# 16-bit sine phases built by doubling, sines in four pieces, and a second written order of the front

## The chip, the cores and the metric

The kernel runs on one NeuronCore of one Trainium2 chip. The metric is the device time of one execution in microseconds, from the first to the last instruction and what lies around them. Lower is better.

## The reference

The inputs are sequences of S = 2048 positions with D = 448 channels in bfloat16. What is computed, cut to what matters:

```python
def _A_ref(q, k, v, shift_k, ssm_k, ssm_D):
    k_shift = sum(k_pad[:, t:t + S, :] * shift_k[:, 3 - t] for t in range(4))    # four taps
    kv = k_shift * v
    y = irfft(rfft(kv_pad, axis=1) * rfft(kf_pad, axis=1))[:S] + kv * ssm_D      # causal convolution, length 4096
    return q * y

x = A_q
h = x + _A_ref(_layernorm(x), A_k, A_v, A_shift_k, A_ssm_k, A_ssm_D)
h2 = h + _B_ref(_layernorm(h), B_w1, B_b1, B_w2, B_b2)    # layernorm, @w1 over S, +b1, gelu, @w2, +b2, transposed
```

## The kernel before

**The Fourier transform as matmuls.** The 2048 positions are laid out as 128 partitions (q) times 16 rows (r). The convolution is done with a two-stage transform. Its factors are sine and cosine values of phases in units of 1/8192 turn. Each factor table is made in the kernel: an integer phase is built on VectorE (DVE), and ScalarE (ACT) takes its sine. The large table is `E`, 128 partitions by 32 times 128 values in float16; its upper half serves rows 8 to 15, its lower half rows 0 to 7. The small tables `FW`, `MA`, `MB`, `MN` serve the second stage and its inverse.

**The steps.** Each operation belongs to a step with a name: the emitting function's tag, a running number, and after a colon the operation's index in the step.
- `dummy`: matmuls without use on PE at the start; `kT.1:9-11` and `kT.3:9-11` are three more each.
- `tables`: `tables.0` iotas on POOL, two memsets and a first Sin activation of one column on ACT (L785); `tables.1` and `tables.3` the identity matrix (L789, L810, L812); `tables.2` further iotas; `tables.4` sixteen memsets on POOL and five operations of up to eight columns on DVE (L822 to L831), the last of which (`tables.4:20`) gives the column scalars that the small tables need; `tables.5` and `tables.6` the phases and the sine of each half of `E` (L837, L841, L844, L847); `tables.7` the small tables (POOL L854 x3 and L858, DVE L860, ACT L862, DVE L866 x2, POOL L871 x3 and L874). After the change the steps that make `E` are `tables.5` to `tables.8`, and the small tables are `tables.9`, with the same indices.
- `loads`: the inputs from HBM: `KN` (A_ssm_k, L887, four transfers), `KH` (A_k, L898, four), `V` (A_v, L901, four), the rest small.
- `kT.0` to `kT.7`: transposes of `KN` on PE (L1037), two steps for each of the four transfers, each copied out of PSUM by an evacuation (L738 on ACT, L741 on DVE).
- `kv.1` to `kv.8`: transposes of `KH` (L965), and their evacuations. `kv.9` to `kv.16`: the four-tap shift as matmuls (L991), each with two multiplications by `V` on DVE (L1006).
- `k1` and `u1` (16 steps each): the first stage (L1058) for the filter and for kv. Each step fills two PSUM banks, is evacuated as 128x896 (L1068; `k1.0` to `k1.3` as an addition on DVE, L1066), and every second step sends three transfers that shuffle partitions, two issued by POOL and one by SP (L1074).
- `k2` and `u2` (8 pairs each): the second stage (L1093), evacuated by ACT or DVE (L739, L742; L738, L741).
- `i1`: 16 products on DVE (L1160), the inverse's matmuls (L1177), their evacuations, and shuffling transfers (L1201, L1188).
- `q`, `xn`: mean and variance of x (`bn_stats` L1237, L1239) and the normalised first rows.
- `ct0`, `ct`: transposes of `E` for the last stage (L1107), each with an evacuation; `ct0` also copies factors (L1126).
- `i2`: the last inverse stage (L1309), the gate, and the second layernorm (L1319 to L1388).
- `mlp`: L1435 and L1445 (w1), Gelu L1425, and L1457 (w2), with the output added on DVE (L1460).

**What sets the order.** The order is written out by hand in `ORDER`: for each of the five engines one list of operations, and an engine works its list from the first to the last. `SLOTS` writes out which of the eight PSUM banks and of the rings of buffers in SBUF each step takes. A planner's model goes through the lists only to emit the instructions; the waits come from what each operation reads and writes. A waiting instruction therefore holds up all that stands behind it on its engine, and transfers stand in the list of the engine that issues them: POOL issues two of three shuffling transfers among its computations. The order about the front's start is, on POOL, `tables.4`'s memsets, `tables.1:0`, `tables.0:1`, `tables.0:2`; on DVE

```
"dummy.0:0 tables.3:0-1 kv.0:3 tables.6:0 tables.4:16 tables.5:0 tables.4:17 tables.6:1 tables.4:18 "
"tables.5:1 tables.4:19 tables.6:2 tables.4:20 tables.5:2 kT.1:8 tables.7:6 kT.0:8 kT.3:8 tables.7:4 "
```

## Time and profile before

| what | value |
|---|---|
| three runs | 170.51, 170.92, 170.98 us; median 170.92 |
| profiled execution, its own time | 170.65 us |
| its span, first to last instruction | 168.8 us |
| granted TensorE clock | 1.000 |
| busy: PE, DVE, ACT, POOL | 160.0, 101.9, 90.4, 58.4 us |

The profiled execution takes 1.85 us more than its span, and the median of the runs is 0.27 us above it. In a row of the timeline stand the start in us, the length, the engine, the line, the operation, the operands' shapes and a count; a merged row holds several equal instructions. In a row of groups stand the count, the busy time in us and the mean of one in ns. In a row of the chain stand start, length, and what was done. In a table by stages stand the stretch, its length, and each engine's busy time.

### The profile page before, as it was taken

What the parts mean: (1) busy time and instruction counts of PE and PEld (TensorE: products, weight loads), DVE (VectorE), ACT (ScalarE), POOL (GpSimd) and SP (SyncE); (2) the same over time, 40 slices, a digit from 0 to 9 for tenths busy, and PEclk for the clock granted to TensorE, in tenths of its full rate; (3) what the DMA queues carried; (4) which work ended last, traced back from release to release, by engine and by line L of the source; (5) the groups of instructions that cost most, each with busy time, mean ns of one, the idle gap of its engine ahead of it and who ended that gap; (6) DMA issues with size and microseconds to landing.
All of it is one profiled execution on the core that took longest, in us unless ns stands there. A gap on an engine that the chain in (4) does not pass through costs nothing.

```text
span 168.8 us, 3562 instructions
## 1 busy us (share of the span) xinstructions
PE 160.0 (95%) x1416; PEld 93.3 (55%) x1416; DVE 101.9 (60%) x191; ACT 90.4 (54%) x130; POOL 58.4 (35%) x155
## 2 busy tenths in 40 slices
...
GB/s 161 407 308 385 270 290 327 329 362 126 222 134 318 248 195 186 208 135 273 388 398 403 424 420 422 415 129 0 0 0 9 50 54 54 54 2 56 54 54 54
DMA packets 15564, 35.15 MB, mean 208 GB/s; under 512 B 3804, under 2 KB 9644, under 8 KB 15548
## 3 DMA queue, kind: packets, MB, share of 16 engines
...
q8 instruction: 11, 0.18, 0.5%
q10 hardware_dynamic: 144, 0.08, 0.2%
...
## 4 chain that ended last, share of the span: by engine, by line
PE 70%; ACT 14%; DMA 5%; DVE 5%; issue 2%; POOL 2%; SPq 0%; DVEq 0%; ACTq 0%
PE ps L1457 25%; PE ps L1435 13%; PE ps L1445 13%; ACT arena L738 7%; DMA arena<-arena 5%; ACT arena L739 4%; PE ps L1309 3%; PE ps L965 3%; ACT arena L1068 3%; PE ps L1024 3%; PE ps L1058 3%; PE ps L1037 3%; DVE arena L1160 2%; POOL arena L1074 2%; PE ps L991 2%
## 5 line engine op out<-in xcount | busy, mean ns | idle before, releaser
L1460 DVE SCALAR_TENSOR_TENSOR arena<-ps,arena 128x448 bf16<-128x448 f32 (+2 forms) x17 | 11.1, 656 | 55.8 <-PE ps L1457 55.8
L1457 PE MATMUL ps<-arena 128*128 128x448 bf16 (+2 forms) x238 | 42.7, 342 | 0.0
L1457 PEld LDWEIGHTS ps<-arena 128*128 128x128 bf16 x238 | 33.3, 145 | 9.5
L1435 PE MATMUL ps<-arena 128*128 128x448 bf16 x112 | 23.5, 353 | 0.0
L738 ACT CAST arena<-ps 128x896 bf16<-128x896 f32 (+1 forms) x29 | 23.1, 933 | 0.0
L1068 ACT CAST arena<-ps 128x896 bf16<-128x896 f32 x24 | 20.2, 919 | 4.1 <-PE ps L1058 3.6
L1445 PE MATMUL ps<-arena 128*128 128x448 bf16 x112 | 22.3, 352 | 0.0
L1074 POOL DMA_DIRECT2D arena<-arena x32 | 17.6, 556 | 7.9 <-ACT arena L1068 7.7
L1425 ACT ACTIVATE arena<-ps,arena 128x448 bf16<-128x448 f32 x14 | 8.2, 632 | 19.3 <-PE ps L1445 10.3
L1093 PE MATMUL ps<-arena 128*64 128x448 bf16 x128 | 15.3, 361 | 1.8 <-ACT arena L739 0.9
L1435 PEld LDWEIGHTS ps<-arena 128*128 128x128 bf16 x112 | 10.7, 98 | 10.6 <-DVE arena L1388 1.1
L1445 PEld LDWEIGHTS ps<-arena 128*128 128x128 bf16 x112 | 11.0, 98 | 10.2
L1160 DVE TENSOR_TENSOR arena<-arena 128x1792 bf16<-128x1792 bf16 x16 | 16.5, 1083 | 0.0
L1177 PE MATMUL ps<-arena 64*128 64x448 bf16 x128 | 14.1, 351 | 1.1 <-ACT arena L738 0.5
L1058 PE MATMUL ps<-arena 128*32 128x448 bf16 x256 | 14.5, 355 | 0.5 <-ACT arena L1068 0.3
L1201 POOL DMA_DIRECT2D arena<-arena x16 | 9.3, 585 | 13.9 <-ACT arena L738 13.0
L1093 PEld LDWEIGHTS ps<-arena 128*64 128x64 f16 x128 | 5.5, 108 | 10.7 <-ACT arena L739 3.4
L1177 PEld LDWEIGHTS ps<-arena 64*128 64x128 f16 x128 | 5.2, 94 | 9.8 <-DVE arena L1160 3.1
L1388 DVE TENSOR_SCALAR arena<-arena 128x448 bf16<-128x448 f32 x16 | 7.6, 509 | 4.8 <-POOL arena L1381 4.8
L1058 PEld LDWEIGHTS ps<-arena 128*32 128x32 f16 x256 | 5.2, 95 | 7.7 <-ACT arena L1068 2.6
L1237 DVE BATCH_NORM_STATS2 arena<-arena 128x6 f32<-128x448 bf16 x16 | 9.4, 613 | 0.0
L739 ACT ACTIVATE arena<-ps 128x896 bf16<-128x896 f32 x10 | 8.6, 926 | 1.1 <-PE ps L1093 1.1
...
## 6 DMA issues: line engine op xcount, KB each, us to landing
...
arena<-arena POOLq DMA_DIRECT2D x32, 112.0 KB, 3.6
...
arena<-in_A_k_dram SPq DMA_DIRECT2D x4, 448.0 KB, 5.8
arena<-in_A_v_dram SPq DMA_DIRECT2D x4, 448.0 KB, 9.2
```

Source lines behind the costliest of these rows:

```text
L738: return e.copy(out=dst(), in_=src())
L739: return e.activation(out=dst(), in_=src(), func=ACT.Copy, scale=scale)
L1058: op("pe", lambda e, W, b=b, r=r, q=q, x=x, c0=c0: e.matmul(PS[32 * q:32 * q + 32, b.slots[x], 0:D], E[:, 2 * r + x, c0:c0 + 32], src[:, r ...
L1068: return e.copy(out=dst, in_=Ppair(b)) if W == "act" else e.tensor_copy(out=dst, in_=Ppair(b))
L1074: shuf[tag].append(op(q_, lambda e, W, g=g, i=i, a=a, nu=nu, jh=jh: e.dma_start(T[a + i:a + i + 4 * nu - 3:4].rearrange("p (j k) c d -> p ...
L1093: op("pe", lambda e, W, b=bs[h], h=h, j=j, c=c, par=par: e.matmul(PS[64 * par:64 * par + 64, b.slots[c], 0:D], FW[:, 64 * c:64 * c + 64], ...
L1160: op("dve", lambda e, W, m=m, i=i: e.tensor_tensor(out=MR(m.slots[0]).rearrange("p (x y) d -> p x y d", x=2), in0=TU[:, i].unsqueeze(2).br ...
L1177: k = op("pe", lambda e, W, b=bs[h], m=ms[h], par=par, t=t, tab=tab, xy=xy, P=P: e.matmul(Pb(b, par), tab[P, :], MR(m.slots[0])[P, xy, :], ...
L1435: op("pe", lambda e, W, r=r, fc=fc, b=bs[fc]: e.matmul(Pb(b), W1A[:, r, 128 * fc:128 * fc + 128], Q[:, r, :], start=(r == 0), stop=(r == R ...
L1445: op("pe", lambda e, W, r=r, fc=fc, b=b: e.matmul(Pb(b), W1B[:, r, 128 * (fc - n0):128 * (fc - n0) + 128], Q[:, r, :], start=(r == 0), sto ...
L1457: op("pe", lambda e, W, r=r, fc=fc, b=b, d0=d0, d1=d1: e.matmul(Pb(b)[:, d0:d1], W2[fc // 7][:, fc % 7, r:S:R], G[:, fc, d0:d1], start=(fc ...
L1460: op("dve", lambda e, W, r=r, b=b, A=A, d0=d0, d1=d1: e.scalar_tensor_tensor(out=XR(r)[:, d0:d1], in0=Pb(b)[:, d0:d1], scalar=bm[:, r:r + ...
```

## The change

- The phases of `E` are 16-bit integers. One POOL iota gives the partition number (`tables.0:0`), two pairs give the frequencies and eight times the frequencies (`tables.0:1` to `tables.0:4`). DVE makes `(q*f & 511) << 4` for row 0 and twice and four times the frequencies; four additions of 128, 256, 512 and 1024 elements then double the number of rows from 1 to 16. For each half three operations of 1024 elements follow: one `and` for the sine's part, an addition and an `and` for the cosine's.
- The sine of each half of `E` is taken in two activations of 1024 elements, where there was one of 2048.
- `ORDER` and `SLOTS` are replaced. SP's list is the same. POOL's transfers stand in the same order among themselves, with other operations between them. On PE, ACT, DVE and POOL the other operations stand in another order up to the early `mlp` steps, and some evacuations go from ACT to DVE or back. `tables.0:5` and `tables.0:6` are now the two memsets and `tables.0:7` the one-column Sin activation, which stands behind `xn` on ACT.

```diff
     "pe": (
-        "dummy.0:1-9 kv.4:0-11 kv.3:0-7 kv.6:0-11 kv.5:0-7 kT.1:0-7 kT.0:0-3 kT.1:9-11 kT.0:4-7 kT.3:0-7 "
-        "kT.2:0-3 kT.3:9-11 kT.5:0-7 kT.2:4-7 ct0.0:0-7 kT.6:0-7 kT.7:0-7 bias.0:0 kv.7:0-7 k1.8:0-7 k1.9:0-7 "
-        "k1.12:0-7 k1.10:0-7 kv.1:0-7 kv.2:0-11 k1.11:0-7 k1.15:0-7 k1.14:0-7 k1.13:0-7 kT.4:0-7 kv.8:0-11 "
-        "kv.12:0-23 kv.9:0-27 kv.10:0-23 kv.11:0-23 k1.4:0-7 kv.11:24-27 k1.0:0-7 u1.0:0-7 u1.1:0-7 k1.1:0-7 "
...
+        "dummy.0:1-9 kv.4:0-11 kv.3:0-7 kv.5:0-7 kT.0:0-3 kv.6:0-11 kT.1:0-7 kT.3:0-7 kT.1:9-11 kT.0:4-7 kT.3:9-11 "
+        "kT.5:0-7 kT.4:0-7 kT.6:0-7 kT.7:0-7 kv.8:0-11 k1.12:0-7 k1.8:0-7 kv.2:0-11 k1.9:0-7 k1.13:0-7 kv.1:0-7 "
+        "kv.7:0-7 k1.10:0-7 k1.11:0-7 kv.12:0-23 kv.9:0-27 k1.14:0-7 k1.15:0-7 kv.10:0-23 kv.14:0-23 kT.2:0-7 "
+        "kv.11:0-27 u1.0:0-7 k1.0:0-7 u1.1:0-7 k1.4:0-7 k1.1:0-7 u1.3:0-7 u1.2:0-7 k1.5:0-7 kv.13:0-27 k1.6:0-7 "
+        "k1.7:0-7 u1.4:0-7 u1.5:0-7 u1.6:0-7 kv.16:0-23 u1.7:0-7 k1.2:0-7 u1.8:0-7 u1.9:0-7 kv.15:0-27 u1.10:0-7 "
+        "k1.3:0-7 k2.4:0-3 k2.5:0-3 k2.12:0-3 k2.13:0-3 u1.12:0-7 u1.13:0-7 u1.11:0-7 k2.9:0-3 k2.8:0-3 u1.14:0-7 "
+        "u1.15:0-7 ct0.0:0-7 k2.0:0-3 k2.1:0-3 k2.6:0-3 k2.7:0-3 k2.3:0-3 k2.2:0-3 k2.14:0-3 k2.15:0-3 u2.0:0-3 "
...
     "act": (
-        "tables.0:5 kv.4:12 kv.3:8 kv.6:12 tables.5:3 tables.6:3 ct0.0:8 bias.0:1 tables.7:5 k1.8:8 k1.9:8 "
-        "k1.10:8 k1.11:8 k1.13:8 k1.14:8 k1.15:8 k1.4:8 u1.0:8 u1.1:8 u1.2:8 u1.4:8 k1.5:8 k1.6:8 k1.7:8 u1.5:8 "
...
+        "tables.6:4 tables.8:4 kv.3:8 kv.5:8 tables.8:3 tables.6:3 k1.12:8 k1.8:8 k1.9:8 k1.13:8 k1.10:8 k1.11:8 "
+        "k1.14:8 k1.15:8 kT.2:8 u1.0:8 u1.1:8 k1.4:8 u1.2:8 k1.5:8 k1.6:8 u1.4:8 u1.5:8 u1.6:8 u1.7:8 tables.9:5 "
+        "u1.8:8 u1.9:8 u1.10:8 k2.5:4 k2.13:4 u1.12:8 u1.11:8 k2.9:4-5 u1.14:8 u1.15:8 k2.1:4 k2.7:4 k2.3:5 k2.15:4 "
+        "u2.1:4 u2.13:5 u2.13:4 u2.11:5 u2.7:5 u2.9:4-5 k2.11:5 k2.11:4 i1.14:18 i1.1:9 i1.14:9 u2.5:4-5 i1.8:18 "
+        "i1.8:9 i1.10:9 i1.10:18 u2.3:5 i1.12:9 i1.12:18 u2.15:5 i1.6:9 i1.6:18 u2.15:4 i1.4:17 i1.4:8 i1.16:18 "
...
     "dve": (
-        "dummy.0:0 tables.3:0-1 kv.0:3 tables.6:0 tables.4:16 tables.5:0 tables.4:17 tables.6:1 tables.4:18 "
-        "tables.5:1 tables.4:19 tables.6:2 tables.4:20 tables.5:2 kT.1:8 tables.7:6 kT.0:8 kT.3:8 tables.7:4 "
-        "tables.7:7 kv.5:8 kT.5:8 kT.2:8 kT.7:8 kT.6:8 bias.1:0 kv.7:8 k1.12:8 kv.1:8 kv.2:12 kv.0:4 kT.4:8 "
...
+        "dummy.0:0 tables.5:0 tables.5:2 tables.5:1 tables.5:4 tables.5:3 tables.5:5-6 tables.3:0 tables.7:0 "
+        "tables.6:1 tables.6:0 kv.4:12 tables.8:0 tables.6:2 tables.8:1 kT.1:8 kv.6:12 kT.3:8 kv.0:3 tables.8:2 "
+        "kT.5:8 kT.4:8 kT.6:8 kT.7:8 kT.0:8 kv.8:12 tables.3:1 kv.2:12 kv.0:4 kv.7:8 tables.4:16 kv.1:8 kv.12:24-25 "
+        "kv.9:29 kv.9:28 kv.10:25 kv.10:24 tables.4:17 kv.14:25 kv.14:24 tables.4:18-19 kv.11:28 tables.4:20 "
+        "kv.11:29 k1.0:8 tables.9:6 k1.1:8 u1.3:8 kv.13:28-29 k1.7:8 q.2:2 kv.16:25 kv.16:24 tables.9:4 k1.2:8 q.1:2 "
+        "kv.15:29 kv.15:28 k1.3:8 k2.5:5 k2.13:5 q.2:3 u1.13:8 tables.9:7 q.1:0 q.1:3 q.1:1 q.2:0-1 q.3:0 ct0.0:8 "
+        "q.3:1 q.4:2 k2.1:5 k2.7:5 k2.3:4 k2.15:5 u2.1:5 i1.0:0 u2.11:4 i1.14:0 u2.7:4 i1.1:0 i1.13:0 i1.10:0 xn.0:1 "
+        "i1.1:18 i1.8:0 i1.7:0 i1.9:0 i1.11:0 i1.5:0 i1.12:0 u2.3:4 i1.6:0 i1.2:0 xn.3:1 i1.3:0 q.5:0 i1.16:0 q.4:0 "
+        "i1.15:0 q.4:3 q.4:1 q.3:2 q.6:2-3 q.3:3 q.5:1 q.6:0 q.5:2 q.6:1 q.5:3 q.8:2 q.7:2 q.8:0 q.7:0 i2.3:0 "
...
     "pool": (
-        "tables.4:0 tables.4:2 tables.4:4 tables.4:6 tables.4:8 tables.4:10 tables.4:12 tables.4:14 tables.4:1 "
-        "tables.4:3 tables.4:5 tables.4:7 tables.4:9 tables.4:11 tables.4:13 tables.4:15 tables.1:0 tables.0:1 "
-        "tables.0:2 tables.0:0 tables.0:3 tables.0:4 loads.13:0 tables.2:0 tables.2:1 tables.2:3 tables.2:5 "
-        "tables.2:7 tables.2:8 tables.2:9 tables.2:10 tables.2:11 tables.2:2 tables.2:4 tables.2:6 q.0:0 q.0:1 "
...
+        "tables.2:9 q.0:1 tables.2:2 tables.0:0 tables.0:3 tables.4:0 tables.2:6 tables.2:0 tables.0:2 tables.4:13 "
+        "tables.4:10 tables.4:12 tables.0:5 tables.0:1 loads.13:0 tables.4:7 tables.4:6 tables.0:4 tables.4:15 "
+        "tables.1:0 tables.2:10 tables.2:7 tables.2:1 tables.2:8 tables.4:8 tables.4:5 tables.2:3 tables.4:2 "
+        "tables.2:4 tables.4:9 tables.4:11 tables.4:14 tables.4:3 kv.0:2 kv.0:0 tables.2:5 tables.4:1 tables.4:4 "
+        "k1.9:9 kv.0:1 k1.9:10 tables.2:11 k1.11:9-10 k1.13:9-10 k1.15:9-10 tables.9:2 tables.9:0-1 u1.1:9-10 "
+        "k1.1:9-10 u1.3:9-10 tables.9:3 k1.5:9-10 u1.5:9-10 k1.7:9-10 u1.7:9 tables.9:8 u1.7:10 u1.9:9-10 k1.3:9-10 "
+        "u1.13:9 q.0:0 u1.13:10 u1.11:9 tables.9:10 q.2:4 q.1:4 tables.9:9 u1.15:10 u1.15:9 u1.11:10 q.1:5 "
+        "tables.9:11 ew.0:0 q.2:5 i1.1:19 i1.1:21 i1.14:19 i1.14:21 i1.8:19 i1.8:21 ew.0:3 xn.3:0 ew.0:2 tables.0:6 "
...
-            o_fr = small(512)
-            o_s = small(64)
+            o_fr = small(256)
+            o_f2, o_f4, o_f8, o_bq = [o_TK + 8192 + 256 * k for k in range(4)]
+            o_s = small(16)
             o_p = small(80)
-            frow = view(o_fr, [128], i32)
-            srow = view(o_s, [16], i32)
+            frow, f2, f4, f8 = [view(o, [128], i16) for o in (o_fr, o_f2, o_f4, o_f8)]
+            qcol = view(o_s, [1], i16)
+            bq = view(o_bq, [128], i16)
...
-            o_pi = o_TT
-            o_nb = o_pi + 8 * HALF
+            o_ph = o_TT
+            o_a1, o_a0 = o_TK, o_TK + 4096
+            ph, a1, a0 = [view(o, [16, 128], i16) for o in (o_ph, o_a1, o_a0)]
+            o_nb = o_ph + 4096
...
-            op("pool", lambda e, W: e.iota(srow, [[1, R]], base=0, channel_multiplier=R), w=[(o_s, 64)])
-            for x in range(2):
-                op("pool", lambda e, W, x=x: e.iota(
-                    frow[:, 64 * x:64 * x + 64].rearrange("p (a b f j) -> p a b f j", a=2, b=2, f=4),
-                    [[2, 2], [4, 2], [64, 4], [8, 4]], base=1 + 32 * x, channel_multiplier=0),
-                   w=[(o_fr, 512, "fr")], n=128, est=160.0)
+            op("pool", lambda e, W: e.iota(qcol, [[0, 1]], base=0, channel_multiplier=1), w=[(o_s, 4)], est=90.0)
+            for m, (dst, o_) in ((1, (frow, o_fr)), (8, (f8, o_f8))):
+                for x in range(2):
+                    op("pool", lambda e, W, x=x, m=m, dst=dst: e.iota(
+                        dst[:, 64 * x:64 * x + 64].rearrange("p (a b f j) -> p a b f j", a=2, b=2, f=4),
+                        [[2 * m, 2], [4 * m, 2], [64 * m, 4], [8 * m, 4]], base=m * (1 + 32 * x), channel_multiplier=0),
+                       w=[(o_, 256, "fr%d" % m)], n=128, est=160.0)
...
-            for h in range(2):
-                sch.t0 = T_TH if h else -40.0
-                o_ph = (o_pi, o_TK)[h]
-                ph = view(o_ph, [2, 8, 128], i32)
-                op("dve", lambda e, W, h=h, ph=ph: e.tensor_tensor(
-                    out=ph[:, 1], in0=frow.unsqueeze(1).broadcast_to([128, 8, 128]),
-                    in1=srow[:, 8 * h:8 * h + 8].unsqueeze(2).broadcast_to([128, 8, 128]), op=ALU.mult),
-                   r=[(o_fr, 512), (o_s, 64)], w=[(o_ph + 4096, 4096)], n=HALF, kind="1x")
-                op("dve", lambda e, W, ph=ph: e.tensor_scalar(
-                    out=ph[:, 0], in0=ph[:, 1], scalar1=2048, scalar2=None, op0=ALU.add),
-                   r=[(o_ph + 4096, 4096)], w=[(o_ph, 4096)], n=HALF)
-                op("dve", lambda e, W, ph=ph: e.tensor_scalar(
-                    out=ph, in0=ph, scalar1=8191, scalar2=None, op0=ALU.bitwise_and),
-                   r=[(o_ph, 8192)], w=[(o_ph, 8192)], n=2 * HALF)
-                op("act", lambda e, W, h=h, ph=ph: e.activation(
-                    out=E[:, 16 * h:16 * h + 16, :].rearrange("p a (b c f) -> p a b c f", b=4, c=2).rearrange("p a b c f -> p (a b) c f"),
-                    in_=ph.rearrange("p c r (g f) -> p c (r g) f", f=16).rearrange("p c g f -> p g c f"),
-                    func=ACT.Sin, bias=bias[:, 0:1], scale=-SC),
-                   r=[(o_ph, 8192), (o_b, 4)], w=[(o_E + 4096 * h, 4096)], n=2 * HALF)
+            sch.t0 = -40.0
+            op("dve", lambda e, W: e.tensor_tensor(out=bq, in0=frow, in1=qcol.broadcast_to([128, 128]), op=ALU.mult),
+               r=[(o_fr, 256), (o_s, 4)], w=[(o_bq, 256)], n=128, est=150.0)
+            op("dve", lambda e, W: e.tensor_scalar(out=ph[:, 0], in0=bq, scalar1=511, scalar2=4, op0=ALU.bitwise_and,
+                                                   op1=ALU.logical_shift_left),
+               r=[(o_bq, 256)], w=[(o_ph, 256)], n=128)
+            for dst, o_, m in ((f2, o_f2, 2), (f4, o_f4, 4)):
+                op("dve", lambda e, W, dst=dst, m=m: e.tensor_scalar(out=dst, in0=frow, scalar1=m, scalar2=None, op0=ALU.mult),
+                   r=[(o_fr, 256)], w=[(o_, 256)], n=128, est=95.0)
+            for m, (fm, o_) in ((1, (frow, o_fr)), (2, (f2, o_f2)), (4, (f4, o_f4)), (8, (f8, o_f8))):
+                op("dve", lambda e, W, m=m, fm=fm: e.tensor_tensor(
+                    out=ph[:, m:2 * m], in0=ph[:, 0:m], in1=fm.unsqueeze(1).broadcast_to([128, m, 128]), op=ALU.add),
+                   r=[(o_ph, 256 * m), (o_, 256)], w=[(o_ph + 256 * m, 256 * m)], n=128 * m)
+                if m < 4:
+                    continue
+                h = m // 4 - 1
+                sch.t0 += 0.1
+                op("dve", lambda e, W, h=h: e.tensor_scalar(
+                    out=a1[:, 8 * h:8 * h + 8], in0=ph[:, 8 * h:8 * h + 8], scalar1=8191, scalar2=None, op0=ALU.bitwise_and),
+                   r=[(o_ph + 2048 * h, 2048)], w=[(o_a1 + 2048 * h, 2048)], n=HALF // 2)
+                op("dve", lambda e, W, h=h: e.tensor_scalar(
+                    out=a0[:, 8 * h:8 * h + 8], in0=ph[:, 8 * h:8 * h + 8], scalar1=2048, scalar2=None, op0=ALU.add),
+                   r=[(o_ph + 2048 * h, 2048)], w=[(o_a0 + 2048 * h, 2048)], n=HALF // 2)
+                op("dve", lambda e, W, h=h: e.tensor_scalar(
+                    out=a0[:, 8 * h:8 * h + 8], in0=a0[:, 8 * h:8 * h + 8], scalar1=8191, scalar2=None, op0=ALU.bitwise_and),
+                   r=[(o_a0 + 2048 * h, 2048)], w=[(o_a0 + 2048 * h, 2048)], n=HALF // 2)
+                for c, (src, o_src_) in enumerate(((a0, o_a0), (a1, o_a1))):
+                    op("act", lambda e, W, h=h, c=c, src=src: e.activation(
+                        out=E[:, 16 * h:16 * h + 16, :].rearrange("p a (b c f) -> p (a b) c f", c=2, f=16)[:, :, c, :],
+                        in_=src[:, 8 * h:8 * h + 8].rearrange("p r (g f) -> p (r g) f", f=16),
+                        func=ACT.Sin, bias=bias[:, 0:1], scale=-SC),
+                       r=[(o_src_ + 2048 * h, 2048), (o_b, 4)], w=[(o_E + 4096 * h, 4096, "E%d" % h)], n=HALF)
+                sch.t0 += 0.1
```

1 line of the change is left out of this document (added), and 126 rows, old and new, of tables (ORDER, SLOTS).

## The prediction

> **What bounds the kernel now.** I read the page first, then a table of busy times by stages, then the chain of waits, then each engine's timeline.
>
> ```profile
> 14.00:36.00 22.00, 21.09 (x446) 12.58 (x447) 20.71 (x33) 17.30 (x22) 14.63 (x29) 1.00 0.92 324
> 36.00:49.90 13.90, 12.65 (x154) 4.93 (x150) 13.51 (x21) 13.45 (x17) 8.72 (x19) 1.00 0.59 190
> 49.90:70.80 20.90, 19.37 (x177) 7.02 (x173) 20.65 (x28) 20.85 (x27) 8.87 (x16) 1.00 0.72 226
> 75.60:166.00 90.40, 90.40 (x488) 57.40 (x489) 29.53 (x73) 24.53 (x53) 14.91 (x39) 1.00 0.45 172
> ```
> ```profile
> 11.80 0.45 PE ps L1107 x8
> 12.25 1.13 PE ps L1037 x16
> ...
> 13.49 0.55 PE ps L965 x8
> 14.05 1.63 PE ps L1058 x32
> ...
> 29.76 0.54 POOL arena L1074
> 30.30 4.45 DMA arena<-arena
> ...
> 34.85 0.97 PE ps L1093 x8
> ...
> 67.89 0.99 DVE arena L1160
> ...
> 68.92 0.95 PE ps L1177 x8
> ...
> 69.89 0.91 ACT arena L738
> ...
> 70.82 0.67 SPq L1188
> ...
> 71.55 3.99 DMA arena<-arena
> ...
> 75.58 2.82 PE ps L1309 x14
> ```
>
> In the table the columns are PE, PEld, DVE, ACT, POOL. From 75.6 us PE works 90.40 us without a gap; nothing there changes in amount, so the time is the start of that stretch plus a constant. The stretch starts when the last shuffle lands (75.54), and its chain goes back to the last product on DVE, which ends at about 68.9. In 36 to 70.8 DVE and ACT are both busy over 96% of the time: they empty PSUM. DVE is also busy 20.71 of 22 us in 14 to 36, where ACT has 4.7 us to spare. An engine's average over the span would hide all this. So **the change is worth what it does to the end of the last product on DVE**, and an early sine is worth something only if it reaches that.
>
> **Part 1: phases and sines, before 14 us.** Old prices, and the load that the first stage also needs (`KN`'s last transfer):
>
> ```profile
> L837 DVE TENSOR_TENSOR arena<-arena 128x1024 int32<-128x1024 int32 x2 | 2.4, 1222 | 0.0
> L844 DVE TENSOR_SCALAR arena<-arena 128x2048 int32<-128x2048 int32 x2 | 2.4, 1226 | 0.0
> L841 DVE TENSOR_SCALAR arena<-arena 128x1024 int32<-128x1024 int32 x2 | 1.4, 691 | 0.0
> L822 DVE TENSOR_TENSOR arena<-arena 128x8 int32<-128x8 int32 x1 | 0.2, 161 | 0.0
> L847 ACT ACTIVATE arena<-arena 128x2048 f16<-128x2048 int32 x2 | 3.9, 2011 | 0.0
> L862 ACT ACTIVATE arena<-arena 128x384 f32<-128x384 int32 x1 | 0.6, 617 | 0.0
> ```
> ```profile
> 1.48 0.60 POOL L779 IOTA arena<- 128x64 int32 x2
> ```
> ```profile
> 0.72 1.28 ACT L785 ACT_TABLE_LOAD   x1 [0.72 <-PEq L1505]
> ```
> ```profile
> 49.91 10.22 DVE L1160 TENSOR_TENSOR arena<-arena 128x1792 bf16<-128x1792 bf16 x10
> ```
> ```profile
> 1.63 2.23 SPq L887 DMA_DIRECT2D arena<-in_A_ssm_k_dram  x4
> ```
> ```profile
> arena<-in_A_ssm_k_dram SPq DMA_DIRECT2D x1, 256.0 KB, 8.4
> ```
>
> Six operations on DVE (2.4+1.4+2.4 = 6.2 us) become fourteen. The trace shows no 16-bit arithmetic of this kind from SBUF. An operation costs at least the 0.16 us of eight elements. For 1024 elements in a scalar operation the upper end is the 32-bit row, 0.69; the lower end halves what lies above 0.16, 0.43. The adds of 128, 256, 512 and 1024 lie likewise between 0.23+0.29+0.43+0.69 and 0.29+0.43+0.69+1.22, and the four small ones cost about 0.2 each. Low sum 1.64+0.8+6x0.43 = 5.0 us, high sum 2.63+0.8+6x0.69 = 7.6 us. I take the low end, since the 16-bit products of 1792 elements (L1160) follow one another every 1.02 us: (1022-161)/1792 = 0.48 ns an element, less than half of L837's (1222-161)/1024 = 1.04.
>
> The Trainium skill, "VectorE: DVE Perf Modes", section "The perf-mode tier table", gives 16-bit scalar operations four elements a cycle and two-tensor ones two; by it 1024 elements would take an estimated 0.43 us, the low end again. No run here shows it yet.
>
> When: in POOL's new list, which starts at 0.7, thirteen operations stand ahead of the last frequency iota. With three 64-wide iotas of 0.3 (0.60/2) and as much again for the rest, memsets of one column and smaller iotas, the frequencies are ready at about 2.4 us; DVE has the first half's phases at 5.5 and the first sine runs from 5.6. A sine of 1024 costs by interpolation 617+640x(2011-617)/1664 = 1153 ns, four 4.6 against 3.9. The last `and` stands on DVE behind the copies of `kv.4`, `kT.1`, `kv.6` and `kT.3`, whose transposes wait for loads; it ends near 11.3, the upper half of `E` is complete at 12.4 (before: 12.6), the lower at 13.4.
>
> That moves little, because the loads do not move. `KN`'s last transfer is issued at about 3.3 and lands 8.4 later, at 11.7; behind it PE has `kT.6`, `kT.7` (1.13) and now `kv.8` (12 transposes at 0.55/8, 0.83). So the first stage starts at 13.65 instead of 14.05: **a gain of 0.4**. PE is ready by then, since `ct0` (0.45), `kT.2` and `kv.7` (about 0.55 each) go behind and `kT.4` and `kv.8` come ahead. At the high price the phases take 2.6 us more, of which 1.3 falls into DVE's wait for `kT.1`; the copies of `kT.4` to `kT.7` queue behind the rest and the start would be about 14.9, a loss of 0.8.
>
> The removed first Sin leaves the table load to the first real sine; if it waits there with its 1.28 us, the first two sines end near 9.4 and the third still waits for 11.3: nothing.
>
> **Part 2: to the second stage.** `pcf` (`tables.4:20`) now stands on DVE behind `kv.11:28`, and POOL's three scalings and its addition, which ran in POOL's empty time at 7.4 to 10.5, stand between shuffles.
>
> ```profile
> arena<-in_A_v_dram SPq DMA_DIRECT2D x1, 448.0 KB, 9.9
> ```
> ```profile
> 20.45 4.38 DVE L1006 TENSOR_TENSOR arena<-ps,arena 128x256 bf16<-128x256 f32 x8
> 24.75 2.08 DVE L1066 TENSOR_TENSOR arena<-ps,arena 128x896 bf16<-128x896 f32 x2
> ...
> 68.78 2.20 DVE L1237 BATCH_NORM_STATS2 arena<-arena 128x6 f32<-128x448 bf16 x4
> ```
> ```profile
> 7.41 2.03 POOL L854 TENSOR_SCALAR arena<-arena 128x128 int32<-128x128 int32 x3 [2.67 <-DVE arena L831]
> 9.53 1.02 POOL L858 TENSOR_TENSOR arena<-arena 128x384 int32<-128x384 int32 x1
> 26.39 3.22 POOL L1074 DMA_DIRECT2D arena<-arena  x6 [4.02 <-ACT arena L1068]
> ```
>
> `V`'s last transfer (issued at 9.75, lands 9.9 later, 19.65) lets DVE start `kv.9`'s multiplications at 19.7. From there it works through `kv.9`, `kv.10`, `kv.14` and half of `kv.11`, seven multiplications of 0.55 (4.38/8), and the small table operations, to 23.9. POOL then takes 2.03 for the scalings, to 26.0, the six issues 3.22 to 29.3, the addition 1.02 to 30.3. `k1.5`'s issue (0.54) and its landing (4.45) follow: 35.3 instead of 34.74, and the first `k2` matmul at 35.45 instead of 34.85: **0.6 late**. Queued behind POOL's wait is every later shuffle. ACT and DVE run out of work at about 35 and stand until `k2` is there; the time is not lost beyond the 0.6, since by then they have done one evacuation (0.82) and `kv.16` (0.9) more than before, less two `bn_stats` (0.55 each).
>
> **Part 3: from there to the last product.** Counted in the two lists, ACT has 41 evacuations left where it had 42. At 22.96/28 = 0.82 each it could be through at 36.4+33.6 = 70.0, with 0.5 of waits 70.5 (before: 70.80).
>
> ```profile
> 47.84 22.96 ACT L738 CAST arena<-ps 128x896 bf16<-128x896 f32 x28
> ...
> 71.60 2.07 ACT L1270 ACTIVATE arena<-arena 128x448 f32<-128x448 bf16 x3
> 73.56 2.06 ACT L738 COPY arena<-ps 128x1024 f16<-128x1024 f16 x2
> ```
> ```profile
> arena<-arena POOLq DMA_DIRECT2D x32, 112.0 KB, 3.6
> ```
>
> DVE sets the end. `i1.0` needs the buffers that the last `u1` shuffles read. Eight evacuations of ACT after 36.4 (6.6) end `u1.15` at 43.0; POOL starts its third issue after that at 44.1; with 3.6 to 4.45 to land, `i1.0` runs from 48.2, against 49.91. Behind it DVE has 16 products (16.4 at 1.02), but now four evacuations (`u2.11:4`, `u2.7:4`, `i1.1:18`, `u2.3:4`; 1.0 each) instead of two, two `bn_stats` (1.1) where there was none, and 0.2 of small ones: 21.7, to 69.9. Before it was 68.86: **1.05 late**. The same from the whole: behind 14.1 us DVE gets `ct0`'s evacuation (0.6) and `tables.3:1`, `tables.4:16-20`, `tables.9:4`, `:6`, `:7` (0.1+0.4+0.3+0.4) and loses `kT.4`'s (0.6), 1.2 us more in a stretch in which it had 1.9 us of gaps (22.0-20.71, 13.9-13.51, 20.9-20.65).
>
> **Part 4: the end.** From the last product the chain is the same 6.7 us. ACT's new order (three `xn` 2.07, a Sin of one column, `ct.1` and `ct.0` 2.06) takes 4.3 us and the last shuffle 4.7 (0.67 and 3.99), so it is hidden; without the wait for the shuffle it would cost 1. `xn.5` and `ct.2` then delay the first gate by 0.6, and `i2.54` and `i2.32` wait for banks that ACT empties: 0.1 on PE.
>
> **Sum.** 170.65 + 1.05 + 0.1 = 171.8 for a profiled execution. The median of the runs stands 0.27 above this one, so **172.1 us**.
>
> **The rivals.**
> 1. *The early sines reach the end: faster.* POOL is free for 4.02 us before 26.39. If `tables.4:20` is through by 22.3, POOL's 3.05 us fit ahead of `u1.1`'s evacuation (25.3), `k1.5`'s shuffle lands at 33.9, `k2` starts at 34.1 when its banks come free, and with DVE's same 33 us behind it the last product ends at 68.1: -0.8, 170.1. For it: that empty time of POOL. Against it: `kv.9` waits for `V` until 19.65 and four steps of `kv` stand between it and `tables.4:20`.
> 2. *POOL's table operations are quick beside DVE.* At 14.29 three POOL operations of two 128-wide inputs took 1.29 us, 0.43 each, while DVE read PSUM:
>
> ```profile
> 14.29 1.29 POOL L871 TENSOR_TENSOR arena<-arena 128x128 f16<-128x128 f32 x3 [3.74 <-ACT arena L862]
> ```
>
> At this price the scalings end 0.7 earlier, `k2` is not late, and about half of it reaches the end: 171.3, no change that can be told. The Trainium skill, "SBUF — State Buffer", section "Who interferes with whom", states why it could be: DVE's two-port operations lock POOL out for a whole instruction, and DVE's PSUM readers do not. Which of the two rows holds here no run shows yet.
> 3. *The 16-bit operations run at the 32-bit price*, so the change does not do what it says: the start is 14.9, 1.2 later than forecast: 173.3.
> 4. *The shuffles of `u1.15` land late*: `u2.10` stands only two pairs behind `u2.0`, before it stood further back. From a landing of 48.7 on both ACT and DVE stand, about 1 us more, and the layernorm behind `ct.2` opens gaps: 173.3.
>
> **How the numbers follow.** About 0.3% (0.5 us) is what a measurement of this kernel can tell from no change. Chances: forecast 0.45, rival 1 0.2, rival 2 0.15, rival 3 0.08, rival 4 0.12. The forecast's own range is 171.2 to 172.9. Down to 170.0 the range takes in rival 1, up to 173.5 rivals 3 and 4. Slower is the forecast, 3 and 4, less the forecast's lower edge: 0.62; the same is rival 2 and that edge: 0.18; faster 0.2.
>
> **What would show it.** In the trace after: DVE's 1024-element operations at 0.43 or 0.69; the last sine ending before 13.5; the first L1058 at 13.65; POOL's L854 row near 24 to 26 and at 0.68 or 0.43 each; the first L1093 at 35.4; the first L1160 at 48.2 and the last ending at 69.9; PE without a gap behind the last landing at 76.6. A last product before 68.4 makes the forecast wrong, and gaps of PE behind 77 would too.

## The result, and the profile after

The median is **173.04 us** over six runs (171.66 to 173.36), against 171.03 for the kernel before in the same comparison. The ratio is 1.0123 with a 95% interval of 1.0098 to 1.0148: the change makes the kernel about 2 us slower. The profiled execution took 171.66 us, with a span of 169.8; it happens to be the shortest of the six, so its trace shows the change at its best, and the experiments had to show the usual case.

The table of busy times by stages, cut at what the prediction steps through: the first stage-1 matmul (L1078, before L1058), the first `k2` matmul (L1113, before L1093), the first product on DVE (L1180, before L1160), the end of the last product, and the start of the matmuls (L1329, before L1309) that wait for the landing of the shuffles and from which PE works to its end. The columns are the stretch, its length, then PE, PEld, DVE, ACT and POOL, the clock, the share of the DMA engines and GB/s. The kernel before:

```profile
13.98:34.85 20.87, 19.96 (x435) 11.74 (x433) 19.71 (x31) 16.80 (x21) 13.49 (x26) 1.00 0.91 321
34.85:49.91 15.06, 13.81 (x164) 5.79 (x164) 14.54 (x24) 13.98 (x18) 9.85 (x22) 1.00 0.63 205
49.91:68.86 18.95, 17.68 (x160) 6.20 (x156) 18.70 (x25) 18.95 (x24) 7.60 (x13) 1.00 0.73 230
13.98:68.86 54.88, 51.46 (x754) 23.73 (x752) 52.96 (x77) 49.73 (x61) 30.95 (x60) 1.00 0.77 258
75.58:166.36 90.78, 90.77 (x491) 57.64 (x491) 29.91 (x74) 24.55 (x53) 14.91 (x39) 1.00 0.44 171
```

The changed kernel, the same view with the same cuts:

```profile
13.19:35.40 22.21, 21.43 (x464) 12.63 (x460) 20.40 (x38) 18.44 (x23) 15.25 (x33) 1.00 0.92 321
35.40:47.86 12.46, 11.09 (x122) 4.40 (x124) 12.40 (x20) 11.78 (x15) 9.73 (x20) 1.00 0.68 223
47.86:69.16 21.30, 19.69 (x184) 7.94 (x184) 21.30 (x26) 21.18 (x26) 10.15 (x20) 1.00 0.67 199
13.19:69.16 55.97, 52.21 (x768) 24.97 (x764) 54.10 (x82) 51.40 (x62) 35.14 (x71) 1.00 0.77 253
75.84:167.38 91.54, 91.23 (x490) 57.06 (x490) 30.31 (x76) 24.91 (x54) 16.48 (x40) 1.00 0.44 170
```

The first stage starts 0.79 us earlier. To the first `k2` matmul it takes 1.34 longer (22.21 against 20.87), and from there to the last product 0.25 less (12.46+21.30 = 33.76 against 34.01). DVE does 1.14 us more between the first stage and the last product (54.10 against 52.96) and is busy all of the last stretch (21.30 of 21.30). The end of PE takes 0.76 more, although its matmuls there are the same: in the last row PE is busy 91.23 of 91.54, before 90.77 of 90.78. So 0.3 of it is idle time; the rest stands inside PE's busy time, and these rows do not show why.

### The profile page after: what moved, and what is told of

It reads as the page before. It is cut to its first block, busy times and chain, and to the rows that moved or that the text cites. A ratio compares the mean times of both kernels' runs of the same rounds, so it can differ in the third digit from the quotient of the medians.

```text
span 169.8 us, 3575 instructions
## 1 busy us (share of the span) xinstructions
PE 159.9 (94%) x1416; PEld 92.7 (55%) x1416; DVE 100.4 (59%) x199; ACT 90.3 (53%) x132; POOL 60.8 (36%) x157
## 4 chain that ended last, share of the span: by engine, by line
PE 52%; DVE 17%; ACT 9%; POOL 9%; DMA 6%; issue 5%; SPq 0%; DVEq 0%; ACTq 0%; POOLq 0%
PE ps L1477 25%; PE ps L1465 12%; DVE arena L1180 9%; ACT arena L1088 5%; PE ps L1455 4%; DMA arena<-in_A_ssm_k_dram 3%; PE ps L1057 3%; POOL arena L1401 3%; DMA arena<-arena 3%; ACT arena L740 2%; DVE arena L742 2%; POOL arena L1094 2%; PE ps L1011 2%; DVE arena L1349 2%; PE ps L1113 2%
## 5 line engine op out<-in xcount | busy, mean ns | idle before, releaser
L1455 PE MATMUL ps<-arena 128*128 128x448 bf16 x112 | 25.2, 353 | 0.3
L1465 PE MATMUL ps<-arena 128*128 128x448 bf16 x112 | 23.3, 353 | 0.0
L1088 ACT CAST arena<-ps 128x896 bf16<-128x896 f32 x25 | 21.1, 915 | 3.0 <-PE ps L1078 2.6
L1094 POOL DMA_DIRECT2D arena<-arena x32 | 17.8, 559 | 6.0 <-ACT arena L1088 3.3
L1113 PE MATMUL ps<-arena 128*64 128x448 bf16 x128 | 15.2, 360 | 2.1 <-ACT arena L739 0.8
L1180 DVE TENSOR_TENSOR arena<-arena 128x1792 bf16<-128x1792 bf16 x16 | 16.7, 1084 | 0.0
L1078 PE MATMUL ps<-arena 128*32 128x448 bf16 x256 | 14.8, 355 | 0.6 <-DVE arena L1026 0.2
L1197 PE MATMUL ps<-arena 64*128 64x448 bf16 x128 | 13.5, 350 | 0.9 <-DVE arena L1180 0.5
L1221 POOL DMA_DIRECT2D arena<-arena x16 | 9.7, 606 | 11.3 <-DVE arena L742 8.6
L1113 PEld LDWEIGHTS ps<-arena 128*64 128x64 f16 x128 | 5.5, 108 | 11.4 <-ACT arena L740 2.2
L1377 ACT ACTIVATE arena<-arena 128x448 bf16<-128x448 f32 x14 | 8.0, 574 | 4.5 <-DVE arena L1349 4.3
L1026 DVE TENSOR_TENSOR arena<-ps,arena 128x512 bf16<-128x512 f32 (+1 forms) x16 | 9.3, 618 | 1.1 <-PE ps L1011 0.9
L742 DVE COPY arena<-ps 128x1024 bf16<-128x1024 bf16 (+2 forms) x14 | 8.6, 648 | 2.1 <-PE ps L1057 1.4
```

Of the source, the lines that this page charges most:

```text
L742: return e.tensor_copy(out=dst(), in_=src())
L1078: op("pe", lambda e, W, b=b, r=r, q=q, x=x, c0=c0: e.matmul(PS[32 * q:32 * q + 32, b.slots[x], 0:D], E[:, 2 * r + x, c0:c0 + 32], src[:, r ...
L1088: return e.copy(out=dst, in_=Ppair(b)) if W == "act" else e.tensor_copy(out=dst, in_=Ppair(b))
L1094: shuf[tag].append(op(q_, lambda e, W, g=g, i=i, a=a, nu=nu, jh=jh: e.dma_start(T[a + i:a + i + 4 * nu - 3:4].rearrange("p (j k) c d -> p ...
L1113: op("pe", lambda e, W, b=bs[h], h=h, j=j, c=c, par=par: e.matmul(PS[64 * par:64 * par + 64, b.slots[c], 0:D], FW[:, 64 * c:64 * c + 64], ...
L1180: op("dve", lambda e, W, m=m, i=i: e.tensor_tensor(out=MR(m.slots[0]).rearrange("p (x y) d -> p x y d", x=2), in0=TU[:, i].unsqueeze(2).br ...
```

## The experiments

Kernels that are compared in one paragraph ran on one chip with the same runs of the kernel before, unless it says otherwise. The changed kernel measured twice, on two chips, gave 1.0123 and 1.0172, so ratios of different occasions are not told apart below about half a per cent.

**The changed kernel again, and its parts.** `e1_again` is the changed kernel with nothing edited. `e2_two_transfers` moves two transfers in POOL's list behind the last product:

```
-q.4:4 i1.16:21-22 q.6:4 q.4:5 q.6:5 i1.4:19 i2.7:0 i1.4:21
+i1.16:21-22 i1.4:19 i1.4:21 q.4:4 q.6:4 q.4:5 q.6:5 i2.7:0
```

`e3_phases_alone` keeps the order of before and takes over only the new phases and the four sines. The new steps stand where the old ones stood (here ACT's list, then DVE's):

```
-tables.0:5 ... tables.5:3 tables.6:3
+tables.0:7 ... tables.6:4 tables.6:3 tables.8:4 tables.8:3
+tables.5:0 5:2 5:1 5:4 5:3 tables.4:16 5:5 4:17 5:6 4:18 6:1 4:19 6:0 4:20 6:2 7:0 8:0-2 kT.1:8
```

> The changed kernel without any edit, for a profile of a typical execution (the one profiled was the shortest of six, 171.66 against a median of 173.04). Theory: the last product on DVE ends at 69.2 as in the profile shown, the bulk of the i2 products starts at 75.8, and what a typical execution has more (1.4 us) lies behind it, in gaps of PE between 76 and 100 us: PE's busy time there falls 1.5 to 2.2 us short of the window. Rival: the typical execution has it earlier, in the first stages: the last product then ends at 70 or later, as forecast, and the i2 bulk starts at 76.6.

> The changed kernel with POOL's two transfers i1.4:19 and i1.4:21 back ahead of q.4:4 and of the power i2.7:0, as they stood before. Theory (these transfers are issued at 74.4 and 77.8 into queues that the weight loads fill, and land late): PE has 0.5 us of gaps or less behind 76, the time falls to 171.4 and varies by 0.3 only. Rival (the gaps come from the order of the layernorm's operations on ACT, DVE and POOL): 172.7 to 173.2 as without the edit; the transfers are then issued at 72 and land before they are wanted in both.

> The new phases and the four sines in the order of before (sines behind the three evacuations on ACT, phases where the old ones stood, the two extra iotas behind POOL's first issue). Theory (the phases themselves cost and bring nothing, because the first stage waits for loads and for PE's transposes): 170.9, within 0.4 of before, first stage-1 matmul at 13.9 to 14.2. Rival (the sines in four pieces or the 16-bit steps cost something by themselves): 171.5 or more. Other rival (earlier sines help): 170.4 or less, the first matmul before 13.7 and the last product before 68.5.

Measured: `e1_again` 173.93 us, 1.0172 (1.0141 to 1.0203). `e2_two_transfers` 173.70, 1.0173 (1.0151 to 1.0194). `e3_phases_alone` 170.48, 0.9982 (0.9960 to 1.0003).

The phases alone cost nothing: **the loss is the new order's**. The two transfers are not its cause either: `e2` takes as long. What the two repeated profiles show is that the first one was lucky in the middle. The theory of `e1`, that the rest lies in gaps at the end, falls: its last product ends at 71.60, not at 69.2. Table of stages of `e1_again`, first stage to `k2`:

```profile
14.74:37.84 23.10, 21.43 (x464) 12.63 (x460) 20.56 (x38) 18.44 (x23) 15.43 (x33) 1.00 0.87 307
```

And of `e2_two_transfers`:

```profile
12.83:36.03 23.20, 21.41 (x464) 12.62 (x460) 20.56 (x38) 18.44 (x23) 15.43 (x33) 1.00 0.92 321
```

And of `e3_phases_alone`, first stage to `k2`, first stage to last product, and the end of PE:

```profile
13.34:34.79 21.45, 20.22 (x435) 11.60 (x433) 20.06 (x32) 17.77 (x23) 13.84 (x27) 1.00 0.93 322
13.34:68.80 55.46, 51.72 (x754) 23.59 (x752) 52.94 (x77) 50.38 (x63) 30.99 (x60) 1.00 0.77 257
75.21:165.99 90.78, 90.78 (x491) 57.62 (x491) 30.09 (x74) 24.83 (x53) 14.95 (x39) 1.00 0.44 171
```

With the new order the middle takes 23.1 to 23.2 us here, not 22.2, with the same work in it (PE 21.4, ACT 18.4 in all three). With the old order it takes 21.45, and the end 90.78, exactly as before. The new phases start the first stage 0.64 us sooner (13.34 against 13.98), of which 0.5 comes from a quicker load (last landing 7.9 us after its issue, before 8.4); little of it is left at the last product (68.80 against 68.86).

**Front and end apart.** `e5_new_front_old_end` has the new order for what starts before 70.8 us and the old one behind; `e6_old_front_new_end` the reverse, both with the new phases. ACT's list about the seam in `e5`, against the changed kernel (PSUM banks behind the seam are assigned anew):

```
-xn.4:0 xn.2:0 xn.1:0 tables.0:7 ct.1:8 ct.0:8 xn.5:0 ct.2:8 i2.46:0 i2.29:0
+ct.0:8 xn.4:0 xn.5:0 xn.2:0 ct.1:8 ct.2:8 i2.46:0 i2.42:0
```

`e7_old_start_new_rest` has `e3`'s order for what starts before 13.5 us, with `tables.4:16-20` and the small tables early, and the new order behind it.

> The changed kernel's order for everything that starts before 70.8 us by the planner, and behind it the order of before on all engines (xn, ct, the gates and the layernorm). In the profiles so far the first k2 matmul stands at 35.4, 37.8 and 36.0 us in three executions of the new order, and the last landing follows 40.5 us behind it each time. Theory A (the start of the second stage carries about two thirds of the loss, the new end the 0.8 us of gaps behind 76): 172.6 to 173.2, PE without gap behind the last landing, the first k2 at 36 to 38. Theory B (the loss is the end's order): 171.2. Theory C (it is the front alone): 173.4 to 173.9 as without the edit.

> The complement: the new phases in the order of before up to 71 us, and behind it the new order of the end. Theory A: 170.5 of the phases alone plus the 0.8 us of gaps, 171.1 to 171.5, PE busy some 0.7 us less than the window between the last landing and 100 us. Theory B: 172.5 or more. Theory C: 170.5, no gaps.

> New phases in the order of before for all that starts before 13.5 us (with it DVE's small table operations and POOL's scalings of the tables, which are then through before the first stage), and the new order behind it to the end. Theory A1 (the new start is what loses: its kT transposes wait for the ssm_k transfers without slack, and the table operations stand between the shuffles): first k2 at 34.9 to 35.8 and not 36 to 38, the time is 171.3 to 171.9, of which 0.8 are the gaps at the end, and its executions lie within 1.3 us as those of before. Theory A2 (the new order between 14 and 36 us loses, whatever lies ahead): first k2 at 36.5 or later, 173 or more.

Measured: `e5` 172.82 us, 1.0114 (1.0074 to 1.0155). `e6` 171.49, 1.0036 (1.0006 to 1.0066). `e7` 173.90, 1.0157 (1.0109 to 1.0204). About two thirds of the loss is the front's and a third, some 0.9 us against `e3`, the end's; for the third the comparison with `e3` goes over two occasions, but the traces bear it out. Table of stages of `e5`:

```profile
13.57:36.59 23.02, 21.43 (x464) 12.64 (x460) 20.57 (x38) 18.44 (x23) 15.45 (x33) 1.00 0.89 310
77.22:168.00 90.78, 90.78 (x491) 57.61 (x491) 30.13 (x74) 24.88 (x53) 14.95 (x39) 1.00 0.44 171
```

Of `e6`, first stage to last product and the end:

```profile
13.38:68.59 55.21, 52.15 (x754) 23.15 (x752) 52.96 (x77) 50.28 (x63) 31.00 (x60) 1.00 0.77 258
74.97:166.91 91.94, 91.33 (x490) 57.18 (x490) 30.16 (x75) 24.85 (x53) 17.15 (x40) 1.00 0.44 170
```

The two losses are separate: with the new front the middle is 23.02 and the end 90.78; with the old front the first is gone and the end is 91.94.

Where the middle's time goes is seen in the chain of waits. The changed kernel at its best (start, length, what was done):

```profile
29.25 4.32 DMA arena<-arena
...
33.64 1.72 ACT arena L1088 x2
...
35.40 0.99 PE ps L1113 x8
```

The same place in `e5`:

```profile
29.63 5.13 DMA arena<-arena
...
34.83 1.72 ACT arena L1088 x2
...
36.59 0.99 PE ps L1113 x8
```

And in `e7`, whose stretch from first stage to `k2` is this row of its table of stages:

```profile
14.92:38.46 23.54, 21.61 (x467) 12.65 (x465) 19.90 (x32) 17.25 (x22) 12.79 (x24) 1.00 0.84 293
```

with this chain at its end:

```profile
31.21 5.46 DMA arena<-arena
...
36.69 1.72 ACT arena L1088 x2
...
38.46 0.57 PE ps L1113 x3
```

The first stage's outputs go through a ring of four buffers in SBUF. `u1.8` takes the buffer of `u1.0` to `u1.3`, so ACT may empty `u1.8` only when the last shuffle that reads that buffer (`u1.3:10`, POOL's sixth issue in a row) has landed; `u1.8` and `u1.9` (1.72 us) hold a PSUM bank that the first `k2` matmul needs. The old order has the same ring, and `u1.8` waits there for the same shuffle, but its landing is in time, and the first `k2` takes the bank of `u1.7`, which ACT empties ahead of `u1.8` (in `SLOTS` bank 4 is `u1.7`'s and then `k2.0`'s; after the change bank 6 is `u1.9`'s and then `k2.4`'s). ACT's timeline of the kernel before:

```profile
29.37 5.80 ACT L1068 CAST arena<-ps 128x896 bf16<-128x896 f32 x7
```

The prediction's row has the six issues from 26.39 to 29.61, so the last of them starts at about 29.07, 15.1 us behind the first stage, and ACT empties seven results without a gap. A DMA stretch of the chain starts with its issue. In the new order that issue starts 16.1 behind the first stage (29.25 less 13.19; 29.63 less 13.57 in `e5`; 16.3 in `e7`), a microsecond later, and the landing is what ACT waits for. It took 4.3, 5.1 and 5.5 us in these three, and 5.3 in `e2`: that is the difference between 22.2 and 23.0 to 23.5. In `e1` the chain names PE's matmuls that end at 36.09 as what released the same two evacuations. By PE's list those are `u1.10`'s, and `u1.8`'s and `u1.9`'s had ended at 34.57. The ring's last shuffle was issued there at 30.82 and landed 5.2 us later, at 36.0, just before ACT starts (row of the DMA issues: KB each, us from issue to landing):

```profile
arena<-arena POOLq DMA_DIRECT2D x1, 112.0 KB, 5.2
```

So the ring fits in all five profiles of this order. `e7`, whose small tables are through early, is no better: they are not what makes this chain late.

**The ring, the extra matmuls, and PE's list at the end.** `e8_six_buffers` gives the ring two more buffers, from memory that is free by then:

```
-gring = _Pool(4)
+gring = _Pool(6)
-o_GR = (o_WR, o_WR + 8 * DB, o_X, o_X + 8 * DB)
+o_GR = (o_WR, o_WR + 8 * DB, o_X, o_X + 8 * DB, o_KH, o_KH + 8 * DB)
-k1.4:8:1 u1.4:8:0 u1.8:8:2
+k1.4:8:4 u1.4:8:5 u1.8:8:0
```

`e11_phases_six_buffers` does that to `e3`. `e9_kv16_u110_later` moves `kv.16` and `u1.10`, which PE does ahead of `k2` in the new order and behind it in the old one, behind the first two pairs (PE's list; their evacuations and multiplications follow):

```
-kv.16:0-23 u1.10:0-7 ... k2.13:0-3
+k2.13:0-3 kv.16:0-23 u1.10:0-7
```

`e10_new_end_old_PE` is `e6` with PE's list of `e3`.

> The changed kernel with six first-stage buffers instead of four (the two more lie where the inputs of kv.3 to kv.6 lay, dead by then; k1.4 to 7 and u1.4 to 7 use them, u1.8 to 11 and u1.12 to 15 take the buffers of k1.12 to 15 and k1.8 to 11). Theory (the first k2 stands 23.0 to 23.2 us behind the first stage-1 matmul because ACT waits ahead of u1.8 for the shuffle of u1.3, issued 5.1 us before, and then empties u1.8 and u1.9 before a PSUM bank is free): the wait of 1.1 us of ACT is gone, the distance is 22.0 to 22.3 us as in the one quick execution, and the time falls by 0.8 to 1.0, to about 173.0 where the unedited order takes 173.9. Rival (PE's own work ahead of k2 sets it, 21.43 us of matmuls against 20.0 in the order of before): distance 23, 173.9.

> The changed kernel with kv.16 and u1.10 behind the first four k2 steps on PE, and their evacuations likewise on DVE and ACT. Theory (buffers): the first k2 can come one evacuation earlier (0.8), but the work only moves behind it, and the last product is not earlier: 173.9 to 175. Rival (PE's work ahead of k2): 1.3 us of matmuls leave the stretch, the first k2 at 21.8 behind the first stage-1 matmul and the time at 172.6.

> The kernel with the order of before up to 71 us and the new order of the end, with PE's list at the end as before as well (each mlp step nearly whole, warm.1 late), so that the new end is only on ACT, DVE and POOL. Theory (PE's interleaved mlp steps ask for the next normalised row before it is ready, so PE waits at L1455 for DVE's L1408): no gap behind the last landing, 170.6. Rival (the new order of the gates and the layernorm on ACT, DVE and POOL makes the rows late): gaps of 0.6 us or more as before the edit, 171.5 or more.

> The new phases in the order of before with six first-stage buffers (k1.0 to 3 and u1.4 to 7 in the two more). Theory: ACT's wait of 0.7 us for a shuffle at 27 is gone, but k2 waits for the landing of its own shuffles too, so the gain is half of it at most: 170.1 to 170.4, not slower than before. Rival: the wait was the bound, and the time falls to 169.8.

Measured: `e8` 173.43 us, 1.0149 (1.0107 to 1.0191). `e9` 175.28, 1.0259 (1.0213 to 1.0305). `e10` 173.17, 1.0148 (1.0114 to 1.0181). `e11` 170.70, 0.9999 (0.9975 to 1.0024).

In `e8` ACT's wait is gone. The middle in its table of stages:

```profile
14.35:36.65 22.30, 21.24 (x464) 12.75 (x461) 20.49 (x38) 18.84 (x23) 15.38 (x33) 1.00 0.87 305
```

Its chain there:

```profile
30.97 1.01 POOL arena L878
31.98 0.49 POOL arena L1094
32.47 3.98 DMA arena<-arena
...
36.65 0.96 PE ps L1113 x8
```

This is the chain that the prediction named: POOL's addition of the small tables (L878) ahead of `k1.5`'s two issues, then the landing of the second. In POOL's timeline the changed kernel has the same:

```profile
29.25 0.54 POOL L1094 DMA_DIRECT2D arena<-arena  x1 [0.32 <-issue]
29.81 1.01 POOL L878 TENSOR_TENSOR arena<-arena 128x384 int32<-128x384 int32 x1
30.76 3.78 POOL L1094 DMA_DIRECT2D arena<-arena  x7
```

There the second issue starts at 30.76+0.54 = 31.30, and its row of the DMA issues gives the landing:

```profile
arena<-arena POOLq DMA_DIRECT2D x1, 112.0 KB, 3.0
```

It landed at 34.3, 1.1 us ahead of `k2`; in `e1`, `e2` and `e5` it took 3.9 to 4.1 us and landed 0.9 to 1.0 ahead. So **a second chain ends about a microsecond ahead of `k2`**, and taking the ring's away leaves it. In the quick execution ACT waited only 0.3 us for the buffer, in `e1`, `e2` and `e5` 1.1 to 1.3. With six buffers the middle took 22.2 to 22.3 us in three profiles (`e8`, `e12`, `e13`), with four 23.0 to 23.5 in four of five. `e8` was expected to be quicker for that, but its time does not show it beyond doubt: 1.0149 against 1.0123 and 1.0172 of the changed kernel on other chips. That the ring costs some 0.8 us in most executions is read from the traces; that its removal saves this much in the median is not shown. In the old order six buffers bring nothing: `e11` was expected at 170.1 to 170.4 and took 170.70, no different from the kernel before.

`e9` answers the rival that the extra matmuls are the cost. The middle is 22.36 with 1.1 us less of PE's work in it, not the 21.8 that the rival asked for. It is 0.7 shorter than the usual 23.1, about the one evacuation that the theory of the buffers gave, and what was moved comes back behind it. Table of stages of `e9`, first stage to `k2` and `k2` to the first product:

```profile
13.51:35.87 22.36, 20.29 (x432) 11.88 (x429) 19.84 (x36) 17.67 (x22) 15.44 (x33) 1.00 0.91 315
35.87:50.79 14.92, 12.45 (x154) 5.29 (x156) 13.22 (x22) 12.72 (x16) 9.64 (x20) 1.00 0.57 187
```

12.46 became 14.92, 2.46 more for 1.14 that was moved. That rival falls: where the two steps stand is right for the rest of this order.

`e10` was to test whether PE's own interleaving makes the gaps at the end. The old list of PE makes the end longer, so the theory falls. Table of stages of `e10`, then PE's timeline, where the brackets give the wait ahead and what ended it:

```profile
75.90:168.97 93.07, 91.23 (x491) 57.69 (x491) 30.33 (x74) 24.74 (x53) 16.54 (x40) 1.00 0.43 168
```
```profile
95.64 1.50 PE L1455 MATMUL ps<-arena 128*128 128x448 bf16 x7 [1.09 <-DVE arena L1408]
```

PE waits 1.09 us for a normalised row. The rows come late because gates and layernorm stand in another order on ACT, DVE and POOL, and PE's new list fits that. In the changed kernel the same wait shows in small pieces (table of waits from 66 to 100 us: who waited for whom, us in total, times, longest):

```profile
DVE arena L1408 <- POOL arena L1401: 3.2, 3, 2.1
PEld ps L1455 <- DVE arena L1408: 2.6, 6, 0.6
```

The kernel before, the same table:

```profile
DVE arena L1388 <- POOL arena L1381: 4.8, 3, 3.2
PEld ps L1435 <- DVE arena L1388: 1.1, 4, 0.3
```

DVE waits less for POOL's power, but PE's weight loads wait more for DVE's rows, 2.6 us against 1.1.

**The small tables ahead.** `e12_tables_first_six_buffers` is `e8` with `tables.4:16-20` ahead of `kT.1:8` on DVE, and POOL's part of the small tables ahead of `k1.9`'s shuffles:

```
+tables.2:5 tables.4:1 tables.4:4 tables.2:11 kv.0:2 tables.9:2 tables.9:0-1 tables.9:3 kv.0:0
```

`e13_same_old_end` is the same with the end of `e5`.

> The changed kernel with six first-stage buffers and, besides, DVE's tables.4:16 to 20 in its wait for kT.1 (7.2 to 8.6 us) and POOL's tables.9:0 to 3 ahead of the shuffles, with the iotas and memsets that they need; the end is the new one. Theory (with six buffers the chain to the first k2 goes over POOL: six issues, the addition of 1.01 us, k1.5's issue and its landing; the addition is the only piece that can go): first k2 21.3 to 21.6 us behind the first stage-1 matmul where it was 22.3, the time 0.7 to 1.0 less, to about 172.5 (1.010 of before). Rival (PE's matmuls, 21.2 us in that stretch, set it as well): distance 22 or more, 173.2 or more.

> The same with the order of before behind 70.8 us. Theory (the loss is made of three pieces that add: the buffers, POOL's table operations between the shuffles, and the end's order, 0.9): 171.5 to 171.8, about 1.005 of before, PE without gaps behind the last landing. If the pieces don't add, because in the new order the stretch from the first k2 on takes the same 33.8 us whatever lies ahead and PE sets its start: 172.2 or more. If it comes out at 170.8 or less, the new order of the stretch between has no cost of its own.

Measured: `e12` 172.48 us, 1.0105 (1.0062 to 1.0147); `e13` 171.97, 1.0087 (1.0057 to 1.0116). The addition is out of the chain, and `k1.5`'s second issue starts a microsecond earlier behind the first stage (at 30.18, 17.08 behind 13.10; in `e8` at 32.47, 18.12 behind 14.35). But it takes longer to land. The middle of `e12` in its table of stages, and then its chain:

```profile
13.10:35.29 22.19, 21.28 (x464) 12.75 (x461) 20.04 (x33) 19.08 (x24) 13.01 (x26) 1.00 0.93 319
```

```profile
28.57 1.61 POOL arena L1094 x3
30.18 4.83 DMA arena<-arena
...
35.29 0.96 PE ps L1113 x8
```

4.83 us where `e8`'s took 3.98, so the middle is 22.19 against 22.30 and not the 21.3 to 21.6 that was expected: in the trace next to nothing is gained. `e12`'s time is what was expected, but it ran on another occasion than `e8` and their intervals overlap, so whether the tables' place matters is not settled. `e13` lies between its two expectations (171.8 or less, 172.2 or more), so whether the pieces of the loss add is not settled either. Its end is 90.79 us, like that of every profile with the old end (90.78 in `e3`, `e5`, `e11` and the kernel before); with the new end it was 91.4 to 93.1 in every one. No kernel here is clearly quicker than the one before; the best is `e3`, 0.9982 (0.9960 to 1.0003).

## Why the prediction was right or wrong

The sign was right, and slower was the likelier answer. The median of 173.04 us lies 0.9 above the forecast of 172.1, just above the forecast's own range (to 172.9) and inside the whole one (to 173.5). It is nearer to the 173.3 of rivals 3 and 4, but what made them slow is not what happened, except for rival 4's gaps. The sum for a profiled execution, 171.8, met the profiled 171.66 by luck: four of its terms missed, two in each direction.

**Part 1 held.** Groups of the changed kernel by form (count, busy us and mean ns, idle ahead):

```profile
L859 DVE TENSOR_SCALAR arena<-arena 128x1024 int16<-128x1024 int16 x2 | 0.9, 442 | 0.0
L849 DVE TENSOR_TENSOR arena<-arena 128x1024 int16<-128x1024 int16 x1 | 0.7, 685 | 0.0
L866 ACT ACTIVATE arena<-arena 128x1024 f16<-128x1024 int16 x4 | 4.4, 1141 | 5.0 <-DVE arena L856 3.6 <-DVE arena L862 1.4
L874 POOL TENSOR_SCALAR arena<-arena 128x128 int32<-128x128 int32 x3 | 1.2, 391 | 1.3 <-DVE arena L837 1.3
```

The scalar operations took 0.44 us where 0.43 was taken, the doubling 0.685 (0.69), a sine 1.141 (1.153). The Trainium skill, "VectorE: DVE Perf Modes", section "The perf-mode tier table", was cited for the low end; the trace agrees, 0.44 and 0.685. ACT's timeline gives the first sine at 5.63 (forecast 5.6) and the last pair's end at 13.18 (13.4):

```profile
0.72 1.28 ACT L866 ACT_TABLE_LOAD   x1 [0.72 <-PEq L1525]
5.63 2.19 ACT L866 ACTIVATE arena<-arena 128x1024 f16<-128x1024 int16 x2 [3.63 <-DVE arena L856]
10.99 2.19 ACT L866 ACTIVATE arena<-arena 128x1024 f16<-128x1024 int16 x2 [1.36 <-DVE arena L862]
```

The first stage started at 13.19 against a forecast of 13.65; `KN`'s last load landed 8.0 us behind its issue and not 8.4, which makes up 0.4 of the 0.46. Rival 3, the 32-bit price, fell.

**Part 2 had the time by luck and missed a chain.** `k2` was forecast at 35.45 and came at 35.40 in the profiled execution, but not for the reason given. The addition was forecast to end at 30.3 and ended at 30.8, and `k1.5`'s shuffle took 3.0 us to land where 4.45 was taken, so it landed at 34.3 and not at 35.3. By that chain alone `k2` could have come a microsecond earlier; ACT's evacuations of `u1.8` and `u1.9` set it, which the ring held up. Behind the first stage 21.8 us was forecast, and it was 22.2 there and 23.0 to 23.5 in four other profiles. The step that failed is the sentence "ACT and DVE run out of work at about 35 and stand until `k2` is there", with one evacuation "more than before" done by then: ACT stands earlier, at `u1.8`, for the ring's buffer, and `k2` waits for ACT. The prediction did not ask which buffer those evacuations write and when POOL has issued the shuffle that frees it; that issue is a microsecond late too. In rival 2 the price was right, 0.39 us a scaling while DVE multiplied out of PSUM. The 0.68 taken in Part 2 was a mean that hid two prices. In POOL's timeline of the kernel before, the first scaling ran beside L844 on DVE, which read and wrote SBUF until 8.43; the other two took 0.36 each behind it, beside a copy out of PSUM:

```profile
7.41 1.33 POOL L854 TENSOR_SCALAR arena<-arena 128x128 int32<-128x128 int32 x1 [2.67 <-DVE arena L831]
```

The Trainium skill, "SBUF — State Buffer", section "Who interferes with whom", is in agreement with these times. The rival's gain did not come, since POOL waited 0.47, 0.20 and 0.32 us ahead of and between the six issues behind the scalings, first for `u1.1`'s evacuation, and the ring's chain ended last. Rival 1, faster, fell with the middle.

**Part 3 was too long by 0.7 us.** From the first `k2` to the last product 34.45 was forecast, 12.75 to the first product and 21.7 of DVE's work; measured were 12.46 and 21.30, 33.76 in all. The statement that DVE sets this end was right (21.30 of 21.30 busy), and the 1.2 us more of DVE's work over the whole came out as 1.14. Rival 4's late shuffles of `u1.15` were not seen: the first product came 0.3 sooner than forecast. Its layernorm gaps were.

**Part 4 failed.** "0.1 on PE" was forecast at the end; 0.76 was measured in the changed kernel's first profile, and 0.6 to 1.6 over the profiles with the new end. The step that failed is the sentence that lets `xn.5` and `ct.2` delay the first gate by 0.6 and counts only 0.1 on PE for all that follows, and with it the start of the prediction, that the stretch behind the landing is a constant: ACT's, DVE's and POOL's lists behind 71 us were not gone through to the last normalised row. The prediction named gaps of PE behind 77 as what would make it wrong, and they are there. `e5` against the changed kernel, `e6` and `e10` put them down to the order of gates and layernorm on those three engines.

In the profiled execution Part 3's 0.7 too much made up for Part 4's 0.7 too little, and Part 1's start, 0.46 too late, for Part 2's stretch, 0.4 too short. The way from there to the median is about 1.4 us, and of it the middle of the usual execution, 0.8 to 1.3 us longer than in the profiled one, can be most. The two repeated profiles differ in the rest: `e1` (2.6 us longer) also starts its first stage 1.6 later, behind a load that took 9.6 us; `e2` (1.8 longer) starts it 0.4 sooner and loses 1.2 behind the last product.

**What stays open.** Which operation at the end makes the rows late. From the last product to the matmuls that wait for the landing, kernels with the new front take 6.7 to 7.7 us, those with the old one 6.3 to 6.7. And first stage to last product still takes 55.9 to 56.0 us in `e8`, `e12` and `e13`, against 54.9 to 55.8 with the old front (56.0 against 55.3 from `e8` to `e11`, where both have six buffers): behind the ring and the tables there may be a remainder of some half a microsecond. Why the ring's last shuffle takes 4.3 us to land once and over 5 in the other profiles was not seen either.
